# First batch of a fused attention and MLP kernel: the next queries' exponentials taken head by head with row sums, and the key maximum moved behind the first gating product

## The chip, the cores and the metric

The kernel runs on one core of one Trainium2 chip. The metric is the device time of one execution in microseconds, as the median of the runs.

## The reference, cut to what matters

Attention without a score matrix comes first, then two MLP blocks. Batch 8, 8 heads of 64 columns, 576 positions. In the part that the change touches, the queries are put through a softmax over the 64 columns of each head, the keys through a softmax over the positions:

```python
q_s = np.exp(q - np.max(q, axis=-1, keepdims=True))
q_s = q_s / (np.sum(q_s, axis=-1, keepdims=True) + 1e-09)
k_s = np.exp(k - np.max(k, axis=2, keepdims=True))
k_s = k_s / (np.sum(k_s, axis=2, keepdims=True) + 1e-09)
kv = np.einsum('bhsd,bhse->bhde', k_s, v)
x = np.einsum('bhsd,bhde->bhse', q_s, kv)
```

The first MLP then takes `h = gelu(x @ w_in)`, splits it into `u` and `v`, layer-normalizes `v`, mixes it over positions with `w_sg`, multiplies by `u` and goes through `w_out`. The second MLP (mixing `U V`, then `w_ch1`, relu, `w_ch2`) takes more than half of the time; the change does not touch it.

## The kernel before, in words

The 576 positions are 5 tiles: four of 128 rows and one of 64. Batches run one after the other in a loop over `b`; while batch `b` is in its first MLP, the queries and keys of batch `nxt = b + 1` are prepared beside it. One pass of the loop has these stages on TensorE, in this order:

- `emit_Vh(b, t)`, t = 0 to 4: the `v` half of `x @ w_in`, into PSUM tile `pv`; ScalarE takes the GELU into `ge` (3 buffers), VectorE the statistics (`stats`), GpSimd the power -0.5, ScalarE scales and copies (`emit_ln`), GpSimd or VectorE takes the low part. Inside this loop stand `q_max` (VectorE) and the steps of `k_fold` (VectorE, four maxima of 128x512 into `km`).
- `k_max(nxt)`: TensorE transposes `km` into `pm`, VectorE reduces it to `mx`.
- `emit_Uh(b, f)`, f = 0 to 3: the `u` half, into `pu`; GELU on ScalarE into `ut`. `pv`, `pu`, `pS`, `py` and `pt` share three PSUM buffers, so the first Uh product takes the buffer of `pv` 2, the second that of `pv` 3, the third that of `pv` 4.
- `k_spread(nxt)`: TensorE spreads `mx` over the partitions into `pb`; `k_sub` on VectorE (5 instructions), `k_exp` on ScalarE (5).
- `q_sub` (VectorE, one tile on GpSimd), `q_exp` (ScalarE, 5 instructions of 512 columns), `q_sum` (VectorE, 5 reductions), `q_total` (VectorE: add, reciprocal), `q_norm` (first two tiles on VectorE, three on GpSimd in the first batch).
- `emit_S(b, f)`, f = 0 to 3: the mixing over positions; VectorE evicts it into `gt` (2 buffers) and multiplies by `ut`; `split_G` copies `gt` to `gh` on ScalarE and takes the low part `gl2` on VectorE.
- `emit_kv(nxt)` needs the exponentials of the keys, `emit_qT(nxt, c)` transposes the normalized queries, then come `emit_y` and `emit_xT(nxt)`.

In the first batch the weights of the first MLP are still being converted from 64-bit words (`Conv`: `stg`, `f`, `wih`/`wil`, `wo_h`/`wo_l`), in slots of the same loop (`slot`, `more`): clamp (L171, VectorE or GpSimd), exponent (L177, ScalarE), merge (L183 and L184, VectorE), split (ScalarE and one of the other two). The Uh products need the sixteenth piece of `w_in` from the third product on.

The order on TensorE and, within the loop, on VectorE is that of the program. The queues of ScalarE, GpSimd and SyncE are laid out at build time by a planner that goes through the program in order and gives an engine the earliest instruction of it that the planner holds to be ready. `tc.issue_after(last['g', 3].ins)` puts instructions behind the GELU of the fourth Uh product on ScalarE: in the first batch the exponentials stand behind it, so that the activation table changes once.

Of the kernel before, what the change touches and what calls it, by code (L numbers as in the profile page):

```python
# [22 lines left out]
def fused_kernel(tc, q, k, v, w_in, g_ln, w_sgT, b_sg, w_out, U, V, w_ch1, w_ch2, outT):  # L23
    nc = tc.nc
    B, S, C = q.shape
    P = 128
# [27 lines left out]
    def tt(eng, out, a, b, op):  # L54
        return eng.tensor_tensor(out=out, in0=a, in1=b, op=op)  # L55
# [358 lines left out]
    def k_max(b):  # L414

        m = km_t.pop(b)
        pm = ps1.tile([P, NC, P], F32, tag="ps1", name="pm")
        for c in range(NC):
            pe.transpose(pm[:, c], m[:, c * P : (c + 1) * P], ident)
        mx = tmpp.tile([P, NC], F32, tag="mx", name="mx")  # L420
        dve.tensor_reduce(out=mx, in_=pm, op=ALU.max, axis=mybir.AxisListType.X)
        kx_t[b] = mx
# [9 lines left out]
    def k_sub(b, t, eng=dve):  # L432
        kt = k_t[b]
        tt(eng, kt[:, t], kt[:, t], kx_t[b], ALU.subtract)

    def k_exp(b, tiles=range(NT + 1)):
        kt = k_t[b]
        for t in tiles:
            act.activation(kt[:, t], kt[:, t], AF.Exp)

    q_s = {}

    def q3(t):
        return qt[0 : TR[t], t].rearrange("p (h d) -> p h d", d=D)

    def q_max(b, t):
        if t == 0:
            q_s[b] = tmpp.tile([P, NT + 1, H], F32, tag="qm", name="qm")
        dve.tensor_reduce(
            out=q_s[b][0 : TR[t], t], in_=q3(t), op=ALU.max, axis=mybir.AxisListType.X  # L450
        )

    def q_sub(b, t, eng=dve):
        n = TR[t]
        tt(eng, q3(t), q3(t), q_s[b][0:n, t].unsqueeze(2).to_broadcast([n, H, D]), ALU.subtract)

    def q_exp(b, t):
        act.activation(qt[0 : TR[t], t], qt[0 : TR[t], t], AF.Exp)

    def q_sum(b, t):  # L460
        if t == 0:
            q_s[b] = tmpp.tile([P, NT + 1, H], F32, tag="qs", name="qs")
        s = q_s[b]
        dve.tensor_reduce(out=s[0 : TR[t], t], in_=q3(t), op=ALU.add, axis=mybir.AxisListType.X)

    def q_total(b):

        s = q_s[b]
        for part in (s[:, 0:NT], s[0:R, NT]):
            dve.tensor_scalar(out=part, in0=part, scalar1=1e-9, scalar2=None, op0=ALU.add)  # L470
            dve.reciprocal(out=part, in_=part)

    def q_norm(b, t, eng=pool):
        n = TR[t]
        tt(eng, q3(t), q3(t), q_s[b][0:n, t].unsqueeze(2).to_broadcast([n, H, D]), ALU.mult)
# [648 lines left out]
    def more(n, lead=1):  # L1124

        with tc.issue_after(gate[0]) if gate else contextlib.nullcontext():
            for _ in range(n):
                if not (pieces or loaded or bounded or begun or merged or stores):
                    if not gate:
                        turn()  # L1130
                    continue
                while pieces and len(loaded) < 3:
                    loaded.append(pieces.popleft())
                    if not loaded[-1].loaded:
                        loaded[-1].load()
                while stores:
                    stores.popleft()()
                if loaded:
                    bounded.append(loaded.popleft())
                    bounded[-1].bound()  # L1140
                if len(bounded) > lead or (bounded and not loaded and not pieces):
                    begun.append(bounded.popleft())
                    begun[-1].start()
                if len(begun) > 1 or (begun and not bounded):
                    merged.append(begun.popleft())
                    merged[-1].merge()
                if len(merged) > 1 or (merged and not begun):
                    merged.popleft().split()

    def run(g):  # L1150
        for _ in g:
            pass
# [34 lines left out]
    OP = (2, 1, 1, 2, 0, 2, 2, 1, 1)  # L1187

    Q_MAX = (((0, 1), (2, 3), (), (4,), ()), ((0, 1, 2), (3,), (4,), (), ()))
    FOLDS = ((0, 1, 2, 1, 0), (0, 0, 2, 2, 0))  # L1190
    Q_SUB = (((0, 1), (2, 3, 4), (), ()),) * 2
    Q_SUB_POOL = ((3,), ())
    K_SUB = (((), (), (0, 1, 2), (3, 4)), ((), (), (0,), (1, 2, 3, 4)))
    Q_NORM_DVE = (2, 5)

    def borrowed(tag):
# [3 lines left out]
    with in_order(dve, act, pool, sp):  # L1200
        load_k(0)
        load_q(0)
        ahead = list(pieces)
        for piece in ahead[0:1]:
            piece.load()
        load_v(0)
        for piece in ahead[1:5]:
            piece.load()
        for piece, tag in zip(ahead[5:14], ("vh0", "vl0", "vh1", "vl1", "vh2", "vl2", "vh3", "vl3", "vh4")):
            piece.load(borrowed(tag))  # L1210
        sp.dma_start(gl, g_ln)
        sp.dma_start(bb, b_sg.partition_broadcast(P))
        run(k_fold(0))
        for t in (0, 1):
            q_max(0, t)
            q_sub(0, t, dve if t in (3,) else pool)
            q_exp(0, t)
        k_max(0)
        for t in range(2, NT + 1):
            q_max(0, t)  # L1220
            q_sub(0, t, dve if t in (3,) else pool)
        k_spread(0)
        for t in range(NT + 1):
            k_sub(0, t)
            k_exp(0, (t,))
            if 0 < t < NT:
                q_exp(0, t + 1)
        more(OP[0])
        emit_kv(0)
        for t in range(NT + 1):  # L1230
            q_sum(0, t)
            if t == 2:
                more(OP[1])
        q_total(0)
        for t in range(NT + 1):
            q_norm(0, t, dve)
            if t == 1:
                more(OP[2])
        norm_kv(0)
        emit_qT(0, 0)  # L1240
        more(OP[3])
        emit_qT(0, 1)
        more(OP[4])
        for c in range(NC):
            emit_xT(0, c)
            if c < 2:
                emit_qT(0, 2 + c)
            more(OP[5 + c])
    gate.append(nc.cur_bb.bb.instructions[-1])
    while gate[-1].engine != act.engine:  # L1250
        gate[-1] = nc.cur_bb.bb.instructions[nc.cur_bb.bb.instructions.index(gate[-1]) - 1]
# [2 lines left out]
    for b in range(B):  # L1254
# [35 lines left out]
                for c in ((), (), (), (0, 1), (2, 3))[t]:  # L1290
                    emit_PV(b - 1, c)

        spread_at = 2 if b else 3
        if nxt:
            k_max(nxt)
        else:
            side["add"] = (dve, pool)
            close_wiv()
            closers = []

            def pool2(key, *args, **kw):
                p2[key], close = opened(key, *args, **kw)
                closers.append(close)

            pool2("uc", side="right")
            prep = u_first()
        late_k = []
        for f in range(NF):
            if nxt and f == spread_at:
                k_spread(nxt)  # L1310
            if b == 0:
                slot(TURNS[b][1][f])
            if not nxt:
                for _ in range((0, 2, 2, 2)[f]):
                    next(prep, None)
            emit_Uh(b, f)
            if f == 0:
                emit_ln(b, NT)
                if nxt:
                    load_v(nxt)  # L1320
                else:
                    next(prep, None)
            if nxt:
                for t in Q_SUB[b > 0][f]:
                    q_sub(nxt, t, pool if t in Q_SUB_POOL[b > 0] else dve)
                for t in K_SUB[b > 0][f]:
                    if f >= spread_at:
                        k_sub(nxt, t)
                    else:
                        late_k.append(t)  # L1330
                if f == spread_at:
                    for t in late_k:
                        k_sub(nxt, t)
            if b > 0:
                slot(TURNS[b][1][f])
        if nxt:
            with contextlib.nullcontext() if b else tc.issue_after(last['g', 3].ins):
                for t in range(NT + 1):
                    q_exp(nxt, t)
            with contextlib.nullcontext() if b else tc.issue_after(last['g', 3].ins):  # L1340
                k_exp(nxt)
            for t in range(NT + 1):
                q_sum(nxt, t)
            q_total(nxt)
            for t in range(NT + 1):
                q_norm(nxt, t, dve if t < Q_NORM_DVE[b > 0] else pool)

        if not nxt:
            close_wiu()
# [2 lines left out]
            chw[0] = ((stgp, 4),) * 4 + ((p2["chx"], 1),)  # L1352
        for f in range(NF):
            emit_S(b, f)
            if not nxt:
                for _ in range((2, 2, 2, 0)[f]):
                    next(prep, None)
            if f > 0:
                split_G(b, f - 1)
            if f == NF - 1:  # L1360
                split_G(b, f)
            slot(TURNS[b][2][f])
# [154 lines left out]
```

## Time and profile before

| | |
|---|---|
| median of 3 runs | 1309.66 us (1308.72 to 1312.9) |
| the profiled execution | 1311.05 us, span 1309.2 us |
| mean granted TensorE clock | 0.991 |
| busy share of the span: PE, DVE, ACT, POOL | 96%, 74%, 49%, 25% |

The stages that matter lie in the first 115 us of the span. Times in the views are counted from the span's start.

### The profile page before, as it was taken

To read this page: it belongs to the slowest core of one execution; us is meant where nothing else is said; L and a number is where in the kernel's file an instruction comes from. 1 tells how busy PE (TensorE), PEld (TensorE's weight loads), DVE (VectorE), ACT (ScalarE), POOL (GpSimd) and SP (SyncE) were. 2 spreads that over 40 slices of the span, in tenths; PEclk is the share of its full clock that TensorE was granted. 3 is DMA by queue.
4 is the path that set the end of the run, shared out by engine and by line. 5 is a ranking of instruction groups with operands and counts; after the bars stand their busy time and mean duration, and the time that the engine had idled before them with its cause. 6 is when DMAs were issued, how large, how long until landed. Compare 5 with 4: busy or idle time off the path is not lost.

```text
span 1309.2 us, 20581 instructions
## 1 busy us (share of the span) xinstructions
PE 1260.0 (96%) x7592; PEld 1139.1 (87%) x7592; DVE 969.0 (74%) x1406; ACT 636.9 (49%) x979; POOL 330.4 (25%) x426
## 2 busy tenths in 40 slices
PE   4799999999999999898999999999999999999998
PEld 3598999999898989798888888888888889999998
DVE  7888879787988888788668953598337963694485
ACT  4756656575757466654454512444134422451342
POOL 4634152624243333665340202000010002000000
PEclk9899999999999999998999999999999999999999
DMA  8515171725343352468998667678756788899896
GB/s 268 164 47 171 37 218 37 225 70 167 96 151 120 111 168 73 162 208 299 312 344 315 227 231 257 209 242 290 257 193 226 243 285 297 269 304 315 260 290 215
DMA packets 135907, 274.14 MB, mean 209 GB/s; under 512 B 15232, under 2 KB 56704, under 8 KB 135808
## 3 DMA queue, kind: packets, MB, share of 16 engines
q1 hardware_dynamic: 135808, 272.84, 63.2%
q8 instruction: 60, 0.98, 0.3%
q14 instruction: 39, 0.32, 0.1%
HBM read 224.56 MB, written 48.23 MB: 208 GB/s over the span
## 4 chain that ended last, share of the span: by engine, by line
PE 79%; DVE 7%; DMA 4%; ACT 2%; issue 1%; POOL 1%; SPq 0%; DVEq 0%; ACTq 0%; POOLq 0%
PE mm L52 50%; PE pS L52 6%; PE pu L52 6%; PE pv L52 5%; PE py L52 5%; DMA stg<-in_w_ch_dram 1%; PE pm L52 1%; PE pp L52 1%; PE px L52 1%; PE pt L698 1%; DVE yt L55 1%; DVE f L183 1%; PE pk L52 1%; PE pt L527 1%; DMA wu<-wd 1%
## 5 line engine op out<-in xcount | busy, mean ns | idle before, releaser
L52 PE MATMUL mm<-oh,wu 128*128 128x512 f32 (+1 forms) x1120 | 320.7, 367 | 0.0
L52 PE MATMUL mm<-uh,wu 128*128 128x512 f32 (+1 forms) x1064 | 303.7, 366 | 1.9 <-DMA wu<-wd 1.1
L52 PEld LDWEIGHTS mm<-oh,wu 128*128 128x128 f32 x1120 | 207.0, 188 | 26.1
L52 PEld LDWEIGHTS mm<-uh,wu 128*128 128x128 f32 x1064 | 196.3, 188 | 26.4 <-issue 1.4
L52 PE MATMUL mm<-ol,wu 128*128 128x512 f32 (+1 forms) x560 | 205.7, 367 | 0.0
L61 ACT ACTIVATE oh<-h 128x1024 fp32r<-128x1024 f32 (+1 forms) x140 | 135.2, 973 | 124.8 <-PE mm L52 102.4
L52 PE MATMUL mm<-ul,wu 128*128 128x512 f32 (+1 forms) x532 | 194.9, 366 | 0.0
L55 DVE TENSOR_TENSOR ol<-h,oh 128x1024 fp32r<-128x1024 f32 (+1 forms) x140 | 155.4, 1113 | 40.9 <-ACT oh L61 40.1
L55 POOL TENSOR_TENSOR ust<-ust 128x1024 f32<-128x1024 f32 (+1 forms) x16 | 36.4, 2282 | 389.4 <-DMA ust<-u2d 348.8
L55 DVE TENSOR_TENSOR h<-mm,u 128x1024 f32<-128x1024 f32 (+1 forms) x57 | 63.3, 1111 | 87.8 <-PE mm L52 87.7
L52 PEld LDWEIGHTS mm<-ol,wu 128*128 128x128 f32 x560 | 105.2, 188 | 13.1
L55 DVE TENSOR_TENSOR u<-mm,u 128x1024 f32<-128x1024 f32 (+1 forms) x53 | 58.9, 1111 | 76.7 <-PE mm L52 71.3
L52 PEld LDWEIGHTS mm<-ul,wu 128*128 128x128 f32 x532 | 99.9, 188 | 12.1
L55 POOL TENSOR_TENSOR chw<-f,chw 128x256 fp32r<-128x256 f32 x98 | 78.9, 820 | 95.4 <-ACT chw L61 95.3
L55 DVE TENSOR_TENSOR h<-h,h 128x1024 f32<-128x1024 f32 (+1 forms) x80 | 88.9, 1112 | 0.0
L1041 ACT ACTIVATE h<-mm 128x1024 f32<-128x1024 f32 (+1 forms) x19 | 17.8, 938 | 130.8 <-PE mm L52 130.8
L1032 ACT ACTIVATE h<-h 128x1024 f32<-128x1024 f32 (+1 forms) x60 | 58.1, 969 | 33.9 <-DVE h L55 33.9
L61 ACT ACTIVATE chw<-f 128x256 fp32r<-128x256 f32 x112 | 42.6, 412 | 62.7 <-DVE f L184 23.1
L61 ACT ACTIVATE u<-mm 128x1024 f32<-128x1024 f32 (+1 forms) x24 | 22.5, 939 | 103.1 <-PE mm L52 86.9
L171 POOL TENSOR_SCALAR stg<-stg 128x256 f32<-128x256 f32 (+1 forms) x83 | 41.0, 496 | 99.7 <-DMA stg<-in_w_ch_dram 39.0
L52 PE MATMUL py<-gh,wo_h 128*128 128x288 f32 x256 | 57.6, 307 | 3.0 <-DVE gt L665 2.1
L52 PE MATMUL py<-gl,wo_h 128*128 128x288 f32 x256 | 56.0, 301 | 3.4 <-DVE gl L55 3.4
(165 smaller groups left out, 2650.2 us busy)
## 6 DMA issues: line engine op xcount, KB each, us to landing
wu<-wd SPq DMA_DIRECT2D x280, 512.0 KB, 4.4
wd<-chw SPq DMA_DIRECT2D x112, 256.0 KB, 3.6
stg<-in_w_ch_dram SPq DMA_DIRECT2D x64, 256.0 KB, 3.7
u2d<-yt SPq DMA_DIRECT2D x32, 288.0 KB, 2.4
vt<-in_v_dram SPq DMA_DIRECT2D x32, 256.0 KB, 6.7
qt<-in_q_dram SPq DMA_DIRECT2D x7, 1024.0 KB, 8.1
kt<-in_k_dram SPq DMA_DIRECT2D x7, 1024.0 KB, 6.1
res<-u2d SPq DMA_DIRECT2D x12, 512.0 KB, 5.3
```

The lines of the kernel that those rows point to most:

```text
L52: pe.matmul(out, lhsT, rhs, start=first, stop=last, skip_group_check=onto)
L55: return eng.tensor_tensor(out=out, in0=a, in1=b, op=op)
L61: return act.activation(out, src, AF.Copy)
L171: eng.tensor_scalar(out=hi, in0=hi, scalar1=F64_MOST, scalar2=-F64_MOST, op0=ALU.min, op1=ALU.max)
L183: dve.tensor_scalar(out=b, in0=b, scalar1=3, scalar2=None, op0=ALU.logical_shift_left)
L527: pe.transpose(pt[:, t * P : (t + 1) * P], qt[:, t, c * P : (c + 1) * P], ident)
L698: pe.transpose(pt[0:n, c * P : (c + 1) * P], y_t[b][:, c, t * P : t * P + n], ident)
L1032: act.activation(h, h, AF.Relu)
L1041: act.activation(h_out(j, 11, n), bank, AF.Relu)
```

## The change: what it does

In the first batch only (`BY_HEAD = {1: ...}`, the queries of batch 1):

- The maximum of the queries is negated, `q_sub` falls away, and `q_exp` becomes 8 instructions of 64 columns for each of the 5 tiles, each with the negated maximum as a per-partition bias and with `accum_out` giving the row sum; `q_sum` falls away. `k_exp` now stands ahead of `q_exp` in the program.
- `q_total` and `q_norm` (`divide`) move from ahead of the first S product to behind the eviction of the third.
- The fold of the keys' maximum moves from the Vh loop to behind the first Uh product, `k_max` from ahead of the first Uh product to behind the third, `k_spread` from ahead of the fourth to behind it, all `k_sub` behind that. `emit_ln` of the last tile moves from the first to the second Uh product.

```diff
+    BY_HEAD = {1: (0, 1, 2, 3, 4)}
...
     def q_exp(b, t):
-        act.activation(qt[0 : TR[t], t], qt[0 : TR[t], t], AF.Exp)
+        if not by_head(b, t):
+            act.activation(qt[0 : TR[t], t], qt[0 : TR[t], t], AF.Exp)
+            return
+        n = TR[t]
+        for h in range(H):
+            x = q3(t)[:, h]
+            act.activation(
+                x, x, AF.Exp, bias=q_m[b][0:n, t, h : h + 1], accum_out=sums(b)[0:n, t, h : h + 1]
+            )
...
-    FOLDS = ((0, 1, 2, 1, 0), (0, 0, 2, 2, 0))
+    FOLDS = ((0, 0, 0, 0, 0), (0, 0, 2, 2, 0))
...
+    def divide(b):
+        for t in range(NT + 1):
+            q_sum(b, t)
+        q_total(b)
+        for t in range(NT + 1):
+            q_norm(b, t, dve if t < Q_NORM_DVE[b > 1] else pool)
...
-        spread_at = 2 if b else 3
+        spread_at = 2 if b else NF
         if nxt:
-            k_max(nxt)
+            if b:
+                k_max(nxt)
...
             emit_Uh(b, f)
+            if b == 0 and f == 0:
+                run(fold)
+            if f == (0 if b else 1):
+                emit_ln(b, NT)
             if f == 0:
-                emit_ln(b, NT)
                 if nxt:
                     load_v(nxt)
...
-            if nxt:
+            if b == 0 and f == 2:
+                k_max(nxt)
+            if nxt and b > 0:
                 for t in Q_SUB[b > 0][f]:
                     q_sub(nxt, t, pool if t in Q_SUB_POOL[b > 0] else dve)
...
         if nxt:
+            if b == 0:
+                k_spread(nxt)
+                for t in range(NT + 1):
+                    k_sub(nxt, t)
+                with tc.issue_after(last['g', 3].ins):
+                    k_exp(nxt)
             with contextlib.nullcontext() if b else tc.issue_after(last['g', 3].ins):
                 for t in range(NT + 1):
                     q_exp(nxt, t)
...
             emit_S(b, f)
+            if b == 0 and f == 2:
+                divide(nxt)
```

## Rows read from the trace of the kernel before

**Rows 1.** The page, busy time of each engine over the whole span.

```profile
PE 1260.0 (96%) x7592; PEld 1139.1 (87%) x7592; DVE 969.0 (74%) x1406; ACT 636.9 (49%) x979; POOL 330.4 (25%) x426
```

**Rows 2.** Waits of PE, 36 to 120 us: total, times, longest.

```profile
PE pm L419 <- DVE km L55: 7.1, 1, 7.1
PE py L52 <- DVE gt L665: 2.1, 1, 2.1
```

**Rows 3.** Windows: length, busy PE, PEld, DVE, ACT, POOL, clock, DMA, GB/s.

```profile
51.70:58.80 7.10, 0.01 (x1) 0.01 (x1) 6.86 (x15) 5.43 (x12) 4.69 (x5) 0.65 0.00 0
58.80:63.90 5.10, 5.10 (x22) 5.10 (x23) 4.62 (x12) 3.70 (x8) 2.36 (x3) 0.50 0.17 55
...
74.90:93.60 18.70, 18.70 (x203) 18.29 (x202) 18.38 (x35) 11.06 (x21) 8.41 (x9) 1.00 0.28 79
```

**Rows 4.** Timeline of PE: start, length, instruction, idle time before it.

```profile
51.31 0.39 PE L52 MATMUL pv<-wil,xr 128*128 128x512 f32 x1
58.79 1.11 PE L419 MATMUL pm<-ident,km 128*128 128x128 f32 x4 [7.09 <-DVE km L55]
...
64.02 0.46 PE L52 MATMUL pu<-xh,wih 128*128 128x288 f32 x2
...
71.24 0.60 PE L429 MATMUL pb<-ident,mx 128*128 128x128 f32 x4
...
74.87 0.43 PE L52 MATMUL pS<-sg_h,vh 128*128 128x288 f32 x2
...
89.87 2.55 PE L52 MATMUL pk<-vt,kt 128*64 128x65 f32 x80
92.36 1.31 PE L527 MATMUL pt<-ident,qt 128*128 128x128 f32 x10
95.72 0.50 PE L52 MATMUL py<-gh,wo_h 128*128 128x288 f32 x2 [2.05 <-DVE gt L665]
```

**Rows 5.** Timeline of DVE, the same columns.

```profile
52.34 1.82 DVE L55 TENSOR_TENSOR km<-km,kt 128x512 f32<-128x512 f32 x2
...
71.88 2.49 DVE L55 TENSOR_TENSOR qt<-qt,qm 128x512 f32<-128x512 f32 x4
...
76.28 3.06 DVE L55 TENSOR_TENSOR kt<-kt,pb 128x512 f32<-128x512 f32 x5
79.27 3.04 DVE L464 TENSOR_REDUCE qs<-qt 128x8 f32<-128x512 f32 x5
82.24 0.16 DVE L470 TENSOR_SCALAR qs<-qs 128x32 f32<-128x32 f32 x1
...
90.25 0.75 DVE L55 TENSOR_TENSOR gl<-gt,gh 128x576 fp32r<-128x576 f32 x1
...
92.77 1.21 DVE L55 TENSOR_TENSOR gt<-gt,ut 128x576 f32<-128x576 f32 x1
```

**Rows 6.** Timeline of ACT, the same columns.

```profile
58.53 0.58 ACT L600 ACTIVATE ge<-pv 128x512 f32<-128x512 f32 x1
...
61.01 0.60 ACT L61 ACTIVATE ge<-pv 64x512 f32<-64x512 f32 x1 [1.39 <-POOL vl L55]
...
77.03 2.72 ACT L458 ACTIVATE qt<-qt 128x512 f32<-128x512 f32 x5
...
81.00 0.41 ACT L177 ACTIVATE f<-stg 128x256 f32<-128x256 f32 x1
...
107.61 0.80 ACT L61 ACTIVATE u_w<-f 128x160 fp32r<-128x160 f32 x3 [1.86 <-DVE f L184]
```

**Rows 7.** Timeline of POOL, the same columns.

```profile
66.01 0.74 POOL L55 TENSOR_TENSOR wil<-f,wih 128x256 fp32r<-128x256 f32 x1
...
82.86 4.80 POOL L55 TENSOR_TENSOR qt<-qt,qs 128x512 f32<-128x512 f32 x3 [1.75 <-DVE qs L470]
```

**Rows 8.** Groups of ACT by form, whole span: count, busy us, mean ns, idle before.

```profile
L623 ACT ACTIVATE ge<-ge,sh,mv 128x512 f32<-128x512 f32 x32 | 26.0, 814 | 17.2 <-DVE sh L620 17.2
...
L600 ACT ACTIVATE ge<-pv 128x512 f32<-128x512 f32 x32 | 19.0, 595 | 25.6 <-PE pv L52 25.6
```

More of the change, by code (lines that the diff above doesn't have):

```diff
@@ L439, in k_exp, with by_head @@
             act.activation(kt[:, t], kt[:, t], AF.Exp)
-    q_s = {}
+    q_m, q_s = {}, {}
+    BY_HEAD = {1: (0, 1, 2, 3, 4)}
+    def by_head(b, t):
+        return t in BY_HEAD.get(b, ())
     def q3(t):
@@ L447, in q_max, with sums, q_total @@
         if t == 0:
[L448 to L451, printed above, removed]
+            q_m[b] = tmpp.tile([P, NT + 1, H], F32, tag="qm", name="qm")
+        o = q_m[b][0 : TR[t], t]
+        if by_head(b, t):
+            dve.tensor_reduce(out=o, in_=q3(t), op=ALU.max, axis=mybir.AxisListType.X, negate=True)
+        else:
+            dve.tensor_reduce(out=o, in_=q3(t), op=ALU.max, axis=mybir.AxisListType.X)
     def q_sub(b, t, eng=dve):
         n = TR[t]
-        tt(eng, q3(t), q3(t), q_s[b][0:n, t].unsqueeze(2).to_broadcast([n, H, D]), ALU.subtract)
-    def q_exp(b, t):
-        act.activation(qt[0 : TR[t], t], qt[0 : TR[t], t], AF.Exp)
+        tt(eng, q3(t), q3(t), q_m[b][0:n, t].unsqueeze(2).to_broadcast([n, H, D]), ALU.subtract)
+    def sums(b):
+        if b not in q_s:
+            q_s[b] = tmpp.tile([P, NT + 1, H], F32, tag="qs", name="qs")
+        return q_s[b]
+    def q_exp(b, t):
+        if not by_head(b, t):
[7 more added lines that the diff above has]
+            )
     def q_sum(b, t):
-        if t == 0:
-            q_s[b] = tmpp.tile([P, NT + 1, H], F32, tag="qs", name="qs")
+        s = sums(b)
+        if not by_head(b, t):
+            dve.tensor_reduce(out=s[0 : TR[t], t], in_=q3(t), op=ALU.add, axis=mybir.AxisListType.X)
+    def q_total(b, first=0, end=NT + 1):
         s = q_s[b]
[L464 to L469, printed above, removed]
+        parts = [s[:, first : min(end, NT)]] if first < NT else []
+        if end > NT:
+            parts.append(s[0:R, NT])
+        for part in parts:
             dve.tensor_scalar(out=part, in0=part, scalar1=1e-9, scalar2=None, op0=ALU.add)
@@ L1189, in fused_kernel @@
     Q_MAX = (((0, 1), (2, 3), (), (4,), ()), ((0, 1, 2), (3,), (4,), (), ()))
-    FOLDS = ((0, 1, 2, 1, 0), (0, 0, 2, 2, 0))
+    FOLDS = ((0, 0, 0, 0, 0), (0, 0, 2, 2, 0))
     Q_SUB = (((0, 1), (2, 3, 4), (), ()),) * 2
     Q_SUB_POOL = ((3,), ())
-    K_SUB = (((), (), (0, 1, 2), (3, 4)), ((), (), (0,), (1, 2, 3, 4)))
+    K_SUB = ((), (), (0,), (1, 2, 3, 4))
     Q_NORM_DVE = (2, 5)
@@ L1322, in fused_kernel @@
                     next(prep, None)
-            if nxt:
+            if b == 0 and f == 2:
+                k_max(nxt)
+            if nxt and b > 0:
                 for t in Q_SUB[b > 0][f]:
                     q_sub(nxt, t, pool if t in Q_SUB_POOL[b > 0] else dve)
-                for t in K_SUB[b > 0][f]:
+                for t in K_SUB[f]:
                     if f >= spread_at:
@@ L1339, in fused_kernel @@
                     q_exp(nxt, t)
-            with contextlib.nullcontext() if b else tc.issue_after(last['g', 3].ins):
+            if b > 0:
                 k_exp(nxt)
[L1342 to L1346, printed above, removed]
+            if b > 0:
+                divide(nxt)
         if not nxt:
@@ L1354, in fused_kernel @@
             emit_S(b, f)
+            if b == 0 and f == 2:
+                divide(nxt)
             if not nxt:
```

## The prediction

> **What bounds the kernel now.** I read the page first: TensorE is busy for 96% of the span [rows 1], so over the whole run only gaps on TensorE, or work done at a low clock, can give time back. The change touches the first batch alone, so I then asked for TensorE's waits in 36 to 120 us. Two stand out: 7.1 us in which the transposes of the keys' maximum wait for VectorE's fold, and 2.1 us in which the first product of y waits for an eviction of VectorE [rows 2]. The windows show what the long wait does beside its length: while TensorE does nothing, the granted clock falls (0.65 over the gap), and for the 5.1 us behind it it is 0.50, the lower level of 1.2 GHz; the stage after that has 1.00, 2.4 GHz [rows 3]. The timeline gives the stations: the last Vh product starts at 51.31, the transposes at 58.79, the first S product at 74.87, the keys' product at 89.87, the query transposes at 92.36, y at 95.72 [rows 4]. In the S stage TensorE never waits, but VectorE is busy for 18.38 of 18.70 us and ScalarE for 11.06 [rows 3]: VectorE is what falls behind, and the 2.1 us before y are its arrears.
>
> **Front part: fold and transposes moved.** The 7.1 us wait goes, since the first Uh product no longer stands behind `km`. What is late next? From 64.02 (the last quarter of the first product) to 71.24 lie two and a quarter products at full clock [rows 4], so one takes 7.2/2.25 = 3.2 us. The first starts at 51.7 and ends at 54.9. The second wants the PSUM buffer of `pv` 3, whose GELU ran at 58.53, 0.58 long; the third that of `pv` 4, whose copy ran at 61.01 with a VectorE add behind it, free at about 62.3 [rows 6]; its last quarter wants the sixteenth weight piece, which GpSimd finished at 66.75 [rows 7]. If none of these moves, the third product ends at 67.5, `pm` (0.6) and the fourth follow, and S starts at 71.5 after `pb`: 3.4 us earlier than 74.87. If nothing waited, four products, `pm` and `pb` from 51.7 give 65.3: 9.6 earlier. They do move somewhat: three maxima of the fold, some 0.9 us each [rows 5], leave VectorE ahead of that GELU, and one query subtraction leaves GpSimd; but ScalarE's own queue sets part of the chain. I take the GELU 1.1 earlier (second product 57.4 to 60.6), the `pv` 4 buffer 1.6 earlier (60.7), the weight piece 2.5 earlier (64.2): third product to 65.0. The fold, four times 0.7 to 0.9 us behind the last statistics, is ready by then or 0.7 us later; `pm` at 65.7, fourth product 66.2 to 69.4, `pb`, S at **70.0: 4.9 us earlier**, between 3.4 and 9.6. The recovered stretch at half clock is in this sum.
>
> **VectorE loses work.** Four subtractions (2.49 us) and five reductions (3.04) go [rows 5]. That would pay if VectorE stayed the one that is late in the S stage. `k_sub` (3.06 us for five) stays, from about 71.
>
> **ScalarE gets it.** Five exponentials in 2.72 us [rows 6] become forty of 64 columns. No row shows one, or a sum output, so it is bounded. Back to back, 512 columns cost (2.72-0.62)/4 = 0.525 us and 160 columns (0.80-0.33)/2 = 0.235 [rows 6], that is 0.82 ns a column and 0.10 fixed; 64 columns cost 0.156. The scaled copy with two pointer operands has 814 ns against 595 for a GELU of the same shape [rows 8]: 0.11 a pointer, so 0.27 with the bias. The sum output costs nothing (0.27 in all, the lower end; no gain is possible), or as much as one further, nearly empty instruction, 0.10 (0.37), or a whole unoverlapped small one, 0.33 less its columns 0.13 and some slack, 0.26 (0.53, the upper end). I take 0.37, as the rows nearest in size overlap: **forty take 14.8 us**, between 10.6 and 21.
>
> A rule of the Trainium skill speaks here, in "ScalarE: Activation LUTs", "What ACT_TABLE_LOAD costs": an ACTIVATE with a pointer bias takes 280 ns and 0.833 ns a column, with 93 ns overlapped back to back. That is 0.24 us for 64 columns and 9.6 for forty, without a price for the sum. The trace agrees on the column (0.82) and cannot show the sum.
>
> When do they end? Before, the exponentials start 2.1 us after the fourth product's end (GELU and table) [rows 4, 6]; now at 71.5. The keys' five come in between (2.72, ready in time from `k_sub`) and a conversion copy (0.4). 71.5 + 2.7 + 0.4 + 14.8 = **89.4**. TensorE is through S and the keys' product at 70.0 + 15.0 + 2.5 = 87.5 [rows 4].
>
> **What waits behind them.** The exponentials are ready as one block as soon as the fourth GELU is out, and they stand in the program ahead of everything of the S stage. The planner gives ScalarE the earliest ready instruction. (Before, a conversion exponent at 81.00 slipped between the keys' exponentials [rows 6], as these waited for VectorE; the queries' wait for nothing.) So the copy `gh` of the first gate falls behind the block; VectorE, in program order, waits for it with the low part of that gate, and behind it stand the third gate and `divide`. From 89.4: copy 0.6, low part to end of the third gate 3.7 (90.25 to 93.98 [rows 5]), total 0.6 (82.24 to GpSimd's start), GpSimd's three normalizations 4.8 [rows 7]: the query transposes start at 99.1, y after 1.3 at 100.4, against 95.72: **4.7 us later**, the 4.9 of the front already counted. Every step of `divide` was covered before by the S products; now TensorE has run out of cover at 87.5 and stands for 11.6 us. That gap is longer than the 7.1 us one, behind which 58.79 to 64.02 ran at half clock, a loss of up to 2.6 us [rows 3, 4]. Part of it falls on transposes that wait for their evictions anyway, so I count 1.6.
>
> **Sum.** -4.9 at S, +9.6 from S to y, +1.6 clock: **+6.3 us**. It is made on the profiled execution (1311.05, span 1309.2); the median of the runs is 1.4 lower, and I put the difference on it: 1309.7 + 6.3 = **1316**. From y on the order is as before and TensorE is the bound, so the shift lasts to the end.
>
> **Rivals.**
> 1. *The copies are not held up* (ends faster). If the planner lets the gates' copies and conversion exponents through the block, `divide` starts when the sums are there: y = block end + 0.6 + 4.8 + 1.3. With 0.27 us each the block ends at 85.2, y starts at 91.9, 3.8 earlier; with a front gain of 6, 5 earlier: 1304 to 1306. It decides below a block end of 89.0; above that even a free order loses. For it: ScalarE has 7.6 us idle in the S stage [rows 3], and exponent 81.00 did slip through. Against: these exponentials are always ready.
> 2. *The exponentials are cheap but block* (about the same). 0.27 to 0.30 each: block end 85.2 to 86.4, y by the long chain at 96.2 to 97.4, +0.5 to +1.7, and up to 1.6 of clock: 1310 to 1313. For it: the lower bound above; against: it leaves no price for the sum. By the figure of the Trainium skill ("ScalarE: Activation LUTs", as above) the block would be 9.6 us long and end at 84.2, for about 1309 to 1311.
> 3. *The sums are dear*: 0.53 each, block end 95.8, y at 106.8, +11, and clock: 1321 to 1323. For it: nothing in the trace shows how a sum leaves ScalarE.
>
> **Chances.** Forecast (slower by 4 to 9) 0.36, rival 1 0.26, rival 2 0.27, rival 3 0.11. The first one's own range is 1312 to 1319; all together give 1303 to 1321, leaving out the best of rival 1 and the worst of rival 3. A measurement of this kernel tells about 0.3%, 3.9 us. Faster by more 0.27, within 0.31 (rival 2, small ends of the others), slower by more 0.42.
>
> **What the profile will show.** Right: no wait of TensorE on `km` before Uh; S starts near 70 with waits on `pv` buffers or weights inside Uh; forty short rows on ScalarE at a pitch of about 0.37 us, followed only then by the first `gh`; VectorE idle ahead of `gl`, TensorE idle ahead of the query transposes for about 10 us, and a low clock behind it. Wrong would be: a pitch under 0.27 or over 0.53, `gh` copies amid the block, S later than 71.5 or earlier than 66, or a query transpose that TensorE reaches without a wait.

## The result, and the profile after

The change makes the kernel slower: **1318.3 us median (1314.83 to 1321.43, seven runs) against 1309.66 (1307.38 to 1314.03), ratio 1.0063, 95% interval 1.0048 to 1.0079**. By the ratio that is 8.3 us, between 6.3 and 10.3; the medians differ by 8.6. The prediction was 1316, range 1303 to 1321, with "slower" the likeliest of the three signs. The profiled execution took 1318.71 us, its span is 1316.9.

The page's first part, for [rows 1]: VectorE gave up 4.4 us of work, ScalarE took 10.3.

```profile
PE 1262.7 (96%) x7592; PEld 1138.9 (86%) x7592; DVE 964.6 (73%) x1397; ACT 647.2 (49%) x1054; POOL 327.8 (25%) x425
```

Waits of TensorE in 36 to 135 us, for [rows 2]:

```profile
PE pt L548 <- DVE qt L55: 6.5, 1, 6.5
PE pt L548 <- POOL qt L55: 2.7, 3, 1.1
PE pu L52 <- POOL wil L55: 2.4, 1, 2.4
PE pm L419 <- DVE km L55: 1.6, 1, 1.6
PE pu L52 <- ACT ge L621: 1.0, 1, 1.0
```

The wait of 7.1 us and the 2.1 us before y are gone. In their place stand three waits in and between the Uh products, 5.0 us together, and 9.2 us of the query transposes. TensorE's timeline for [rows 4]:

```profile
53.08 0.40 PE L52 MATMUL pv<-wil,xr 128*128 128x512 f32 x1
...
57.67 0.53 PE L52 MATMUL pu<-xh,wih 128*128 128x288 f32 x2 [1.02 <-ACT ge L621]
...
66.47 0.53 PE L52 MATMUL pu<-xh,wil 128*128 128x288 f32 x2 [2.42 <-POOL wil L55]
...
68.63 1.11 PE L419 MATMUL pm<-ident,km 128*128 128x128 f32 x4 [1.63 <-DVE km L55]
69.39 0.83 PE L52 MATMUL pu<-xh,wih 128*128 128x288 f32 x2
...
73.85 0.60 PE L429 MATMUL pb<-ident,mx 128*128 128x128 f32 x4
74.20 0.51 PE L52 MATMUL pS<-sg_h,vh 128*128 128x288 f32 x2
...
89.29 2.55 PE L52 MATMUL pk<-vt,kt 128*64 128x65 f32 x80
98.37 0.99 PE L548 MATMUL pt<-ident,qt 128*128 128x128 f32 x2 [6.52 <-DVE qt L55]
...
102.97 1.54 PE L548 MATMUL pt<-ident,qt 128*128 128x128 f32 x6 [1.04 <-POOL qt L55]
104.16 0.83 PE L52 MATMUL py<-gh,wo_h 128*128 128x288 f32 x2
```

This execution reached the last Vh product (the last matmul of Vh) 1.8 us later than the one of before: its clock was 0.57 from 41 to 45 us. Such a stretch (0.61 to 0.63) is also in the profiles of experiments 4, 7, 8 and 12, with and without the moved fold, and not in the others, so I count from the start of the last Vh product. To S: 21.1 us, before 23.6, 2.4 earlier by this count. From S to y: 30.0, before 20.9, **9.1 lost**.

The count flatters the front part, because only TensorE was late. Experiment 3 is the same program up to S and had no such stretch: its last Vh product starts at 51.79, 1.3 us earlier than here. But ScalarE's scaling copy of `ge` comes at 54.22 there and at 53.62 here, and the third Uh product gets GpSimd's sixteenth weight piece at the same time of the span, 66.46 and 66.47. ScalarE and GpSimd here, then TensorE in experiment 3:

```profile
53.62 0.82 ACT L644 ACTIVATE ge<-ge,sh,mv 128x512 f32<-128x512 f32 x1
```

```profile
65.70 0.71 POOL L55 TENSOR_TENSOR wil<-f,wih 128x256 fp32r<-128x256 f32 x1
```

```profile
66.46 0.53 PE L52 MATMUL pu<-xh,wil 128*128 128x288 f32 x2 [1.81 <-POOL wil L55]
```

In the span S starts at 74.20 instead of 74.87, **0.7 earlier**.

The windows, for [rows 3] (length, busy PE, PEld, DVE, ACT, POOL, clock, DMA, GB/s):

```profile
68.60:73.80 5.20, 5.17 (x28) 5.17 (x29) 3.37 (x7) 1.66 (x3) 0.00 (x0) 0.67 0.15 45
...
74.90:93.60 18.70, 16.95 (x189) 16.64 (x187) 7.34 (x15) 18.69 (x91) 2.06 (x5) 1.00 0.17 50
91.90:98.30 6.40, 0.00 (x0) 0.00 (x0) 4.62 (x12) 4.23 (x12) 2.94 (x4) 0.82 0.11 26
98.30:104.40 6.10, 3.31 (x11) 2.17 (x12) 5.09 (x5) 0.92 (x2) 4.61 (x3) 0.50 0.02 4
```

VectorE and ScalarE have changed places: in the S stage ScalarE is now busy all the time, VectorE for 7.34 of 18.70 us. Behind the waits the granted clock is lower: 0.67 over the fourth Uh product and 0.50, the lower level of 1.2 GHz, over the transposes. ScalarE's timeline, for [rows 6]:

```profile
76.02 0.35 ACT L475 ACTIVATE qt<-qt,qm 128x64 f32<-128x64 f32 x1
76.27 0.18 ACT L475 ACTIVATION_READ_ACCUMULATOR qt<-qt,qm 128x1 f32 x1
76.36 0.33 ACT L475 ACTIVATE qt<-qt,qm 128x64 f32<-128x64 f32 x1
...
91.81 0.19 ACT L475 ACTIVATION_READ_ACCUMULATOR qt<-qt,qm 64x1 f32 x1
91.90 0.40 ACT L61 ACTIVATE wo_h<-f 128x256 fp32r<-128x256 f32 x1
92.21 0.41 ACT L177 ACTIVATE f<-stg 128x256 f32<-128x256 f32 x1
92.53 0.40 ACT L61 ACTIVATE wo_h<-f 128x256 fp32r<-128x256 f32 x1
92.84 0.67 ACT L61 ACTIVATE gh<-gt 128x576 fp32r<-128x576 f32 x1
```

Each exponential is two instructions, the second reads its sum. The block lasts 15.88 us; without the keys' five inside it (0.52 each) that is 13.28, or 0.332 for one of forty. Two conversion copies, an exponent, and then the first `gh`. VectorE, for [rows 5], waits for it:

```profile
62.84 5.74 DVE L55 TENSOR_TENSOR km<-km,kt 128x512 f32<-128x512 f32 x3
...
93.53 0.87 DVE L55 TENSOR_TENSOR gl<-gt,gh 128x576 fp32r<-128x576 f32 x1 [9.99 <-ACT gh L61]
...
96.86 0.17 DVE L491 TENSOR_SCALAR qs<-qs 128x32 f32<-128x32 f32 x1
```

and GpSimd's normalizations, for [rows 7], come 14.6 us later than before:

```profile
97.49 5.42 POOL L55 TENSOR_TENSOR qt<-qt,qs 128x512 f32<-128x512 f32 x3 [1.17 <-DVE qs L491]
```

### The profile page after: what moved, and what is told of

Read it like the earlier page. It is cut to its first block, busy times and chain, and to the rows that moved or that the text cites. A ratio compares the mean times of both kernels' runs of the same rounds, so it can differ in the third digit from the quotient of the medians.

```text
span 1316.9 us, 20655 instructions
## 1 busy us (share of the span) xinstructions
PE 1262.7 (96%) x7592; PEld 1138.9 (86%) x7592; DVE 964.6 (73%) x1397; ACT 647.2 (49%) x1054; POOL 327.8 (25%) x425
## 4 chain that ended last, share of the span: by engine, by line
PE 75%; DVE 9%; ACT 6%; DMA 5%; issue 2%; POOL 2%; SPq 1%; DVEq 0%; ACTq 0%; POOLq 0%
PE mm L52 50%; PE pv L52 5%; PE pS L52 5%; PE pu L52 4%; PE py L52 4%; DMA stg<-in_w_ch_dram 1%; DVE f L183 1%; DMA qt<-in_q_dram 1%; PE pp L52 1%; DVE yt L55 1%; ACT qt L475 1%; PE px L52 1%; PE pt L719 1%; DVE f L184 1%; DVE ul L55 1%
## 5 line engine op out<-in xcount | busy, mean ns | idle before, releaser
L61 ACT ACTIVATE chw<-f 128x256 fp32r<-128x256 f32 x112 | 42.7, 412 | 62.5 <-DVE f L184 22.8
L52 PE MATMUL pu<-xh,wih 128*128 128x288 f32 x256 | 57.0, 304 | 2.1 <-ACT ge L621 1.0
```

The costliest lines, as they stand in the source:

```text
L52: pe.matmul(out, lhsT, rhs, start=first, stop=last, skip_group_check=onto)
L61: return act.activation(out, src, AF.Copy)
```

## The experiments

All stations in one table, from the timelines of TensorE: us from the start of the last Vh product to the first S product, and from there to y. The ratio is the recorded one, each against runs of the kernel before made beside it; it differs from the ratio of the two medians by up to 0.0007. The last column is this ratio less one, times 1309.7 us.

| kernel | to S | S to y | both, less before | ratio (95% interval) | us |
|---|---|---|---|---|---|
| before | 23.6 | 20.9 | | | |
| changed | 21.1 | 30.0 | +6.7 | 1.0063 (1.0048 to 1.0079) | +8.3 |
| 1 moved fold alone | 24.2 | 20.1 | -0.1 | 0.9999 (0.9987 to 1.0011) | -0.1 |
| 2 heads alone | 22.2 | 30.7 | +8.5 | 1.0067 (1.0051 to 1.0082) | +8.8 |
| 3 copies let through | 23.8 | 30.7 | +10.1 | 1.0066 (1.0053 to 1.0080) | +8.6 |
| 4 whole tiles | 24.6 | 23.3 | +3.6 | 1.0025 (1.0013 to 1.0037) | +3.3 |
| 5 two tiles by head | 25.3 | 25.5 | +6.4 | 1.0059 (1.0037 to 1.0080) | +7.7 |
| 6 copies, division earlier | 23.9 | 28.4 | +7.8 | 1.0058 (1.0045 to 1.0071) | +7.6 |
| 7 transposes alone | 24.8 | 20.2 | +0.6 | 1.0007 (0.9994 to 1.0020) | +0.9 |
| 8 subtractions early | 22.9 | 20.3 | -1.3 | 1.0006 (0.9994 to 1.0018) | +0.8 |
| 9 maximum early | 21.3 | 23.3 | +0.2 | 1.0002 (0.9992 to 1.0012) | +0.3 |
| 10 no sums | 22.8 | 26.3 | +4.7 | 1.0032 (1.0022 to 1.0042) | +4.2 |
| 11 norms on GpSimd | 22.6 | 24.0 | +2.1 | 1.0004 (0.9995 to 1.0013) | +0.5 |
| 12 one tile by head | 19.1 | 22.2 | -3.1 | 0.9988 (0.9978 to 0.9999) | -1.6 |

The stations come from one execution each. Up to S the changed kernel and experiments 3, 6 and 10 are the same program with the same order on every engine, and yet S comes 21.1, 23.8, 23.9 and 22.8 us after the last Vh product (22.9 on average, 0.7 less than before); 9 and 11 are the same up to S too, with 21.3 and 22.6. So a difference of up to some 3 us ahead of S isn't shown by one pair of profiles.

The theory was the prediction's: the block on ScalarE holds the gates' copies, VectorE stands in program order, and so the division comes late. Its rivals: the late place of `divide` does it by itself; or the moved fold costs something.

**1. The moved fold alone** (the kernel before, with the fold, the transposes, the keys' broadcast and subtractions and the last tile's layer norm at their new places):

```
-    FOLDS = ((0, 1, 2, 1, 0), (0, 0, 2, 2, 0))
+    FOLDS = ((0, 0, 0, 0, 0), (0, 0, 2, 2, 0))
...
             emit_Uh(b, f)
+            if b == 0 and f == 0:
+                run(fold)
...
+            if b == 0 and f == 2:
+                k_max(nxt)
...
+            if b == 0:
+                k_spread(nxt)
+                for t in range(NT + 1):
+                    k_sub(nxt, t)
```

> The kernel before with the fold, the transposes and the spread of the keys' maximum moved, and the queries as before (whole tiles, subtraction and sums on VectorE, divided ahead of the first S product). Theory A (ScalarE's block of forty exponentials costs the time, the front part gives 2 to 3 us): S starts 2 to 3 us earlier than before, y 0 to 2 us earlier since VectorE is still in arrears; median 1307 to 1310, ratio to before 0.998 to 1.000. Theory B (the moved fold, which runs against GpSimd, and the low clock behind its gap are what costs): slower than before by 3 us or more, ratio 1.002 to 1.006.

1309.0 us: no gain at all. The timeline of TensorE shows the 7.1 us split into three:

```profile
58.57 0.53 PE L52 MATMUL pu<-xh,wih 128*128 128x288 f32 x2 [2.85 <-ACT ut L645]
66.35 0.53 PE L52 MATMUL pu<-xh,wil 128*128 128x288 f32 x2 [1.40 <-POOL wil L55]
69.90 1.12 PE L419 MATMUL pm<-ident,km 128*128 128x128 f32 x4 [3.02 <-DVE km L55]
```

2.85 + 1.40 + 3.02 = 7.3 us. S is 0.7 us later than before.

**2. Heads alone** (the changed kernel, with fold, transposes, broadcast, keys' subtractions and layer norm at their old places):

```
-    FOLDS = ((0, 0, 0, 0, 0), (0, 0, 2, 2, 0))
+    FOLDS = ((0, 1, 2, 1, 0), (0, 0, 2, 2, 0))
...
-        spread_at = 2 if b else NF
+        spread_at = 2 if b else 3
         if nxt:
-            if b:
-                k_max(nxt)
+            k_max(nxt)
```

> The changed kernel with fold, transposes, spread and key subtractions back at their old places; exponentials head by head with sums and the late division stay. Theory A: the 7 us gap before Uh is back, S starts near 74.9, the block of exponentials ends near 92 and y starts at 104 to 106; ratio to before 1.006 to 1.009. Theory B: within 2 us of before, ratio 0.999 to 1.002.

1317.6 us, +8.8: the whole loss without the moved fold. The long wait for `km` is there again (6.8 us), and yet S comes 1.4 earlier than before by the count. That isn't VectorE's doing: from the transposes to S TensorE waits for nothing in either kernel. Most of it (1.1 us) is the clock, which stays at half speed for 2.8 us behind the wait here (59.70 to 62.50) and for 5.2 before (58.79 to 64.02).

**3. Copies let through** (the exponentials of the last three tiles stand between the S products; `divide` behind them):

```
-                for t in range(NT + 1):
+                for t in range(NT + 1 if b else 2):
                     q_exp(nxt, t)
...
             emit_S(b, f)
-            if b == 0 and f == 2:
-                divide(nxt)
...
             slot(TURNS[b][2][f])
+            if b == 0 and f < 3:
+                with tc.issue_after(last['g', 3].ins):
+                    q_exp(nxt, 2 + f)
+            if b == 0 and f == 3:
+                divide(nxt)
```

> The changed kernel with the exponentials of the last three query tiles put into the program between the S products, so that gate copies and conversions of ScalarE go ahead of them, and the division behind the fourth S product. Theory A in the form put on record (the copies held up by the block cost some 5 us of the way from the block's end to y): y starts 2 to 4 us earlier than in the changed kernel, ratio to before 1.003 to 1.005, VectorE's 10 us wait for the first gate copy gone. Theory C (the length of the block and GpSimd's late normalizations alone set y): y within 1 us of the changed kernel, ratio 1.005 to 1.008.

1317.42 us, nothing won. VectorE's timeline:

```profile
89.61 0.76 DVE L55 TENSOR_TENSOR gl<-gt,gh 128x576 fp32r<-128x576 f32 x1 [4.69 <-ACT gh L61]
...
99.49 0.17 DVE L491 TENSOR_SCALAR qs<-qs 128x32 f32<-128x32 f32 x1
```

VectorE's wait halved, but what slipped in pushed the end of the last exponential back to 96.0; the division, here behind all four low parts, starts at 99.5. (y is 3.4 us further from the last Vh product than in the changed kernel, 2.1 further in the span, with the same median. Why was not tried; one difference is that there the last gate's low part comes at 104.73, behind the start of y, and here all four are done before it.)

**4. Whole tiles** (the changed kernel with five exponentials of whole tiles, subtractions and sums on VectorE; moved fold and late `divide` stay):

```
-    BY_HEAD = {1: (0, 1, 2, 3, 4)}
+    BY_HEAD = {}
...
+            if b == 0:
+                for t in Q_SUB[0][f]:
+                    q_sub(nxt, t, pool if t in Q_SUB_POOL[0] else dve)
```

> The changed kernel with the exponentials as five whole tiles again, subtraction and sums on VectorE (one subtraction on GpSimd); the moved fold and the late division (behind the third gate) stay. Theory A: the exponentials end near 82, the division is done by 94 and y starts at 93 to 96; ratio to before 0.996 to 1.001. Theory C (late division with GpSimd's normalizations uncovered costs whatever the exponentials do): y not before 99, ratio 1.003 to 1.007. Theory B: ratio over 1.003, with S not before 74.

1312.72 us, +3.3. Against the first experiment the place of `divide` differs, with VectorE's sums in it, and the keys' exponentials stand ahead of the queries' in the program; but ScalarE takes the queries' first in both traces (79.51 here, 77.70 there). So the late division costs about 3.4 us with whole tiles too, and the heads the other 5.0. With the division at 94.1 the query transposes wait for GpSimd, 3.1 us in three parts.

**5. Two tiles by head:**

```
-    BY_HEAD = {1: (0, 1, 2, 3, 4)}
+    BY_HEAD = {1: (0, 1)}
```

(with the subtractions of the other three as above)

> The changed kernel with two of the five query tiles by head (16 small exponentials) and three as whole tiles with subtraction and sum on VectorE. Theory A (the length of ScalarE's block sets the way from S to y): the block is 6 us shorter than in the changed kernel, the way from S to y 24 to 27 us, against 30 with five tiles by head; ratio to before 1.002 to 1.005. Theory C (the late division costs by itself, the number of small exponentials hardly matters): the way from S to y 28 us or more, ratio over 1.005.

1317.26 us. From S to y it lies between 4 and the changed kernel, nearer to 4 (25.5); but with the subtractions back, two of them on VectorE, S is as late as in 4, 4.2 us behind the changed kernel. Its seven runs lie between 1310.44 and 1321.23, too far apart to place it between 4 and the changed kernel by time.

**6. Copies let through, division earlier** (as 3, with `divide` right behind the fourth eviction of S):

```
-            if b == 0 and f == 2:
+            if b == 0 and f == 3:
                 divide(nxt)
```

> The kernel with the exponentials of the last three tiles put between the S products, and the division now directly behind the eviction of the fourth S product, ahead of the low parts of the gates. If the place of the division was what hid the gain in the run with the division behind them: the sums end at 96 as there, the transposes of the queries start 3 us earlier, y near 103, 27 to 28 us after S; ratio to before 1.004 to 1.005. If ScalarE's length alone counts: y at 105 or later, ratio 1.006 to 1.007.

1316.13 us: the query transposes start 3.1 us earlier than in 3 (97.91), the median is 1.3 lower, inside the intervals. The order of the copies isn't what can be won back.

**7. Transposes alone** (as 1, with the fold at its old place):

```
-    FOLDS = ((0, 0, 0, 0, 0), (0, 0, 2, 2, 0))
+    FOLDS = ((0, 1, 2, 1, 0), (0, 0, 2, 2, 0))
...
-            if b == 0 and f == 0:
-                run(fold)
```

> The kernel before with the fold at its old place in the Vh loop and only the transposes, spread and key subtractions moved; queries as before. Theory A with the fold's collision (the fold behind the first Uh product runs against GpSimd and takes 6 us in place of 3, so the third product is followed by a wait of 3 us and a low clock): no wait on the fold, S starts 22 us or less after the last Vh product (24.2 with the moved fold), y 18 to 20 us after S; ratio 0.997 to 1.000. If the buffers of pv and the weights set the Uh stage alone: S starts 24 us after, ratio 0.999 to 1.001.

1310.5 us. No wait for `km`, but TensorE's next wait took its place:

```profile
77.76 0.65 PE L429 MATMUL pb<-ident,mx 128*128 128x128 f32 x4 [3.45 <-DVE mx L421]
```

VectorE does the maximum `mx` behind the last tile's layer norm and the query subtractions.

**8. Subtractions early** (as 7, the query subtractions ahead of that layer norm):

```
+            if b == 0 and f == 0:
+                for t in range(NT + 1):
+                    q_sub(nxt, t, pool if t in Q_SUB_POOL[0] else dve)
             if f == (0 if b else 1):
                 emit_ln(b, NT)
```

> As the run with the transposes alone moved, and the query subtractions put right behind the first Uh product, ahead of the layer norm of the last tile, into stretches in which VectorE waited for ScalarE and GpSimd. If VectorE's arrears in the S stage set y: y 2 us earlier than with the transposes alone; ratio to before 0.995 to 0.999. If not: the same as with the transposes alone.

1309.03 us, the same as before. By the stations y comes 1.3 earlier, less than they vary by themselves, and a wait for `yt` of 1.69 us at 106.0 (0.60 before) stands behind it.

**9. Maximum early** (as 8, with `k_max` behind the second product, ahead of the layer norm):

```
-            if b == 0 and f == 2:
+            if b == 0 and f == 1:
                 k_max(nxt)
```

> The kernel before with the queries as before and the fold at its old place, the query subtractions early (as in the run before), and the transposes of the keys' maximum behind the second Uh product instead of the third, with their maximum on VectorE ahead of the last tile's layer norm. Theory A (the moved wait of 7.1 us only splits up, because ScalarE's GELUs and GpSimd's weight piece are late for the Uh products whatever the transposes do): the 3.2 us wait of `pb` for `mx` goes, the waits of `pu` for ScalarE and for the weight piece (2.5 and 1.4) stay, S starts 20 to 21 us behind the start of the last Vh product instead of 23.6, y 20 to 21 us later; 1306 to 1308, that is 1.5 to 3.5 us below the kernel before. Theory B (VectorE's order after the statistics is the chain, and any place of the maximum is paid for by arrears behind it): S at 22 to 24, y waits again for evictions; 1308.5 to 1311.

1309.86 us. Now S does start 2.2 us earlier (1.0 in experiment 11, which is the same up to S), with a wait for `mx` of only 0.35. TensorE's timeline behind S:

```profile
92.08 0.77 PE L527 MATMUL pt<-ident,qt 128*128 128x128 f32 x5
93.56 0.77 PE L527 MATMUL pt<-ident,qt 128*128 128x128 f32 x5 [0.71 <-DVE gt L665]
96.42 0.50 PE L52 MATMUL py<-gh,wo_h 128*128 128x288 f32 x2 [2.10 <-DVE gt L665]
```

The gates are where they were. VectorE's arrears set y here, whatever TensorE wins in front.

**10. No sums** (the changed kernel; the row sums are left out and set to one, the division stays):

```
-                x, x, AF.Exp, bias=q_m[b][0:n, t, h : h + 1], accum_out=sums(b)[0:n, t, h : h + 1]
+                x, x, AF.Exp, bias=q_m[b][0:n, t, h : h + 1]
```

> The changed kernel with the forty exponentials without their row sums: the sums are left out of the computation (set to one), the divisions by them stay. Theory A (the length of ScalarE's block sets when the gate copies, the division and the query transposes come): the pitch of an exponential falls from 0.33 to 0.24 us (0.10 fixed and 0.82 ns a column give 0.15 without the bias, the row of the exponential up to the sum's own row lasts 0.24), the block shortens by 40 x 0.09 = 3.6 us, VectorE's wait for `gh` from 10.0 to about 6.4, y comes 3.6 us earlier: 1314 to 1315.5. Theory B (the place of the division and GpSimd's normalizations set it, not the block): y moves by less than 1 us; 1317 to 1319. If the sum output costs nothing by itself and the pitch is that of the bias, the pitch stays 0.33 and the time too.

1314.58 us, 4.1 less than the changed kernel by the ratios. ScalarE's and then VectorE's timeline:

```profile
76.61 5.14 ACT L477 ACTIVATE qt<-qt,qm 128x64 f32<-128x64 f32 x21
```

```profile
90.45 0.91 DVE L55 TENSOR_TENSOR gl<-gt,gh 128x576 fp32r<-128x576 f32 x1 [6.30 <-ACT gh L61]
```

5.14/21 = 0.24 us for one; the wait for `gh` fell from 9.99 to 6.30, the stretch from S to y by 3.7. The block's length passes on to y one to one.

**11. All normalizations on GpSimd** (as 9):

```
-    Q_NORM_DVE = (2, 5)
+    Q_NORM_DVE = (0, 5)
```

> The run before (maximum early) with all five normalizations of the next queries on GpSimd instead of two on VectorE. Theory A (behind S VectorE's arrears set y: waits of 0.7 and 2.1 us of TensorE on its gates): VectorE loses 1.24 us, the gates and y come about 1.2 us earlier, 1307.5 to 1309, about 1 us under the kernel before; GpSimd starts at about 83.7 and needs five times 1.6 = 8 us, so it is done at 91.7, just ahead of the query transposes. Theory B (GpSimd becomes the late one, as its products are up to 1.8 us each while VectorE works): a query transpose waits 1 to 3 us for GpSimd, y is not earlier; 1309.5 to 1312.

1310.79 us, no gain, but not as the rival had it: no transpose waits for GpSimd, whose five take 5.85 us. VectorE itself is slowed by them:

```profile
86.97 1.13 DVE L183 TENSOR_SCALAR f<-f 128x256 uint32<-128x256 uint32 x1
88.13 1.15 DVE L184 SCALAR_TENSOR_TENSOR f<-stg,f 128x256 uint32<-128x256 uint32 x1
89.20 1.13 DVE L171 TENSOR_SCALAR stg<-stg 128x256 f32<-128x256 f32 x1
90.26 1.13 DVE L183 TENSOR_SCALAR f<-f 128x256 uint32<-128x256 uint32 x1
```

A row of L183 lasts 0.29 us in the same trace with GpSimd idle (77.46). From the first of these rows to the next gate on VectorE 5.2 us pass (86.97 to 92.18), in experiment 9 3.1 (86.41 to 89.51): 2.1 us lost for the 1.24 taken off.

**12. One tile by head** (placement of 9, the division at its old place; only the first of five tiles head by head):

```
-    BY_HEAD = {1: (0, 1, 2, 3, 4)}
+    BY_HEAD = {1: (0,)}
...
-            if b == 0 and f == 2:
-                divide(nxt)
```

> The same placement (maximum early, fold and division at their old places), with only the first of the five query tiles head by head, its row sums from ScalarE. Theory A (the change's trade pays in a small dose, as ScalarE has 7 us to spare in the S stage and VectorE none): VectorE loses one subtraction and one reduction, 1.3 us; ScalarE gets 8 x 0.33 - 0.52 = 2.1 us more, its exponentials end at about 85, before the first gate is there; y about 1.3 us earlier than in the run before, 1307.5 to 1309. Theory B (any exponential head by head delays the copies of the gates or the division behind it by what it adds): the keys' exponentials and the conversions slip by 2.1 us, y is not earlier or up to 2 us later; 1309.5 to 1312.

1308.39 us against 1310.38, ratio 0.9988 with an interval that ends at 0.9999: the one version whose interval lies below 1, by a hair. TensorE's timeline:

```profile
72.04 0.60 PE L429 MATMUL pb<-ident,mx 128*128 128x128 f32 x4
72.39 0.51 PE L52 MATMUL pS<-sg_h,vh 128*128 128x288 f32 x2
...
94.62 0.50 PE L52 MATMUL py<-gh,wo_h 128*128 128x288 f32 x2 [2.12 <-DVE gt L686]
```

S to y is 1.0 us shorter than in 9, where 1.3 was expected of a subtraction and a sum less. The other 2.3 us, ahead of S, are mostly not real. The second Uh product waits 2.6 us for its buffer instead of 4.0, but only because TensorE came 1.5 us later (last Vh product at 53.34 against 51.85, clock 0.61 from 41 to 45): the wait ends at the same time in both. TensorE in 9 and here:

```profile
59.43 0.53 PE L52 MATMUL pu<-xh,wih 128*128 128x288 f32 x2 [3.99 <-ACT ut L645]
```

```profile
59.46 0.85 PE L52 MATMUL pu<-xh,wih 128*128 128x288 f32 x2 [2.60 <-ACT ut L666]
```

In the span S starts 0.8 earlier than in 9 (`pb` no longer waits for `mx`, with one subtraction fewer ahead of it) and y 1.8 (94.62 against 96.42), as much as the ratios differ. With twelve versions tried, one interval that just misses 1 can be chance.

## Why the prediction was right, and where its sizes were off

**The mechanism held, but for one link.** The exponentials run as one block, the first `gh` comes only behind them, VectorE waits 9.99 us for it, the third gate and `divide` behind it, the query transposes late, and a low clock behind that. Experiments 1, 2 and 4 put the cause where the prediction did: the heads and the division behind them are the whole loss. The link that doesn't carry weight is the held-up copy: with the copies let through (3 and 6) VectorE's wait for `gh` is half as long, 4.69 us, and the time is the same within the intervals. What counts is when the sums end and the division after them.

From S to y +9.6 was predicted and +9.1 is in the profile. Its terms were off by more: the block ended 17.7 us behind S where 19.4 was counted, but two conversion copies and an exponent went ahead of `gh` (0.9) and GpSimd's normalizations took 5.42 instead of 4.8. And TensorE didn't stand for 11.6 us in one piece: the prediction had all query transposes wait for GpSimd, while the first two, on tiles that VectorE normalizes, started at 98.37; the waits are 6.5 and 2.7 us.

**The exponential** was 0.332 us, not 0.37: inside the bounds, 1.5 us less for forty. Experiment 10 splits it: 0.24 with the pointer bias (0.27 was my estimate) and 0.09 for the sum (0.10 taken, as one nearly empty instruction). The Trainium skill ("ScalarE: Activation LUTs", "What ACT_TABLE_LOAD costs") gives 0.24 us for 64 columns by the estimate quoted in the prediction; the trace without sums agrees, and the sum is what it left out.

**The front part was mis-sized, and this step failed.** S was to come 4.9 us earlier, at 70.0, at the least 3.4. It came at 74.20, 0.7 earlier in the span, and the other executions with the same order up to S (10, 3 and 6) have it at 74.81, 75.57 and 76.09: 0.3 later on average by the span, 0.7 earlier by the count, so about nothing was gained. S later than 71.5 was also among the prediction's signs against it. The 4.2 us lie in three terms. The GELU of `pv` 3 did come earlier as predicted (second product at 57.67, 57.4 was forecast), but the sixteenth weight piece, counted 2.5 us earlier at 64.2, was done at 66.4 where it had been at 66.75, so the third product ended 2.0 late. The fold, counted at four times 0.7 to 0.9 us, took 6.4 us (62.13 to 68.5) with GpSimd at work beside it to 68.0, and `pm` lost another 0.9. And from `pm` to S it took 5.6 us instead of 4.3, as the fourth product, costed at full clock, ran at 0.67 behind the new waits (69.39 to 73.85, 4.5 us for 3.2): "the recovered stretch at half clock is in this sum" didn't hold. The moved fold alone gives no gain either (1).

**The clock behind the gap**, put at +1.6, was about +0.3. The first four groups of y run slowly (104.16 to 106.21, 2.05 us against 1.1 before), but waits inside y that the kernel before had take 0.6 of it back: from y to the third group of transposes it is 7.4 us (111.52) against 7.1 before.

**The sum**, in times of the span: -0.7 + 9.1 + 0.3 = +8.7, where -4.9 + 9.6 + 1.6 = +6.3 was predicted. The profiled pair differs by 7.7, the medians by 8.6. The front was 4.2 too good, the other two terms 1.8 too bad; that the total came so close is in part luck.

**The rivals.** Rival 1 (copies not held up, faster): experiments 3 and 6 let the copies through, and nothing is won, as the prediction's point of decision says (a block end of 89.0; it was 91.9 in the changed kernel). Rival 2 needed 0.27 to 0.30 an exponential; only without sums (10) is it there, and then the time is 1314.6, slower than its 1310 to 1313, as the front gain was too small. Rival 3 fell on the price.

**What the prediction did not see** is that the late place of `divide` costs 3.4 us even with cheap whole-tile exponentials (4), and that neither half of the change paid alone: the moved transposes run into VectorE's arrears (9), and the heads that would relieve VectorE fill ScalarE. A small dose of both (12) measured 1.6 us better, between 0.1 and 2.9, the one gain among twelve versions and not repeated.

## What to carry to other kernels

Work that goes from a late engine to one with idle time is priced by what stands behind it in the new engine's queue, not by the idle time: here 7.6 us of idle ScalarE took on 10.6 us more, and VectorE, which was to be relieved, waited 10 us for a copy behind it. Before a wait is removed, look for the next one on the same chain: a 7.1 us wait fell into three of the same sum. And try such work in small portions: one tile of five, with the division at its old place, lost nothing and gained perhaps 1.6 us, where five with the late division lost 8.3.

## What the runs showed of the hardware

- A row sum from ScalarE is an instruction of its own behind the exponential: its row is 0.19 us long, and it adds 0.09 to the pitch. The groups of ScalarE in the changed kernel, 74.9 to 93.6 us (count, busy us, mean ns):

```profile
L475 ACT ACTIVATE qt<-qt,qm 128x64 f32<-128x64 f32 x32 | 10.6, 334 | 0.0
L475 ACT ACTIVATION_READ_ACCUMULATOR qt<-qt,qm 128x1 f32 x32 | 6.0, 187 | 0.0
...
L475 ACT ACTIVATE qt<-qt,qm 64x64 f32<-64x64 f32 x8 | 2.7, 333 | 0.0
```

  Sixty-four partitions cost as much as 128 (333 against 334 ns).
- VectorE and GpSimd slow each other. The changed kernel's fold, by tile:

```profile
L55 DVE TENSOR_TENSOR km<-km,kt x3: 796/1652/3220, 62.8 to 65.4; 128x512 f32<-128x512 f32 x3
```

  One maximum of two 128x512 tiles took 0.80, another 3.22 us, both beside GpSimd's work. GpSimd's three normalizations took 5.42 us beside VectorE and 3.03 in experiment 3, where VectorE was done. The Trainium skill ("SBUF — State Buffer", "Who interferes with whom") says that a VectorE instruction with two inputs in SBUF contends with a GpSimd instruction that reads SBUF, and that the 2-port modes contend too; the rows with two inputs agree. The one-input rows of experiment 11 (0.29 us alone, 1.13 beside GpSimd) fit it only if they run in such a mode, which no row shows. Nor does any run here show which of the two engines holds the other.
